# Other places for stores, modulation rows and attention parts in a transformer block on one NeuronCore

## The chip, the core and the metric

The kernel runs on one core of a Trainium2 chip. The core has five engines that run side by side: TensorE (PE, matrix products; its weight loads are listed as PEld), VectorE (DVE), ScalarE (ACT), GpSimd (POOL), and SyncE (SP), which here issues all DMAs. The metric is the device time of one execution in microseconds, less is better.

## The reference

One transformer block on 2048 tokens of 1024 channels in float32. A vector c gives six modulation rows, x is normalised and modulated, goes through a memory-augmented attention with 32 heads of 32 channels in four segments of 512 tokens, and then through a GEGLU feed-forward of 3584 channels:

```python
mod = (silu(c) @ w_mod).reshape(6, D)          # sa, ca, ga, sb, cb, gb
h = layernorm(x) * (1 + ca) + sa
q, k, v = h @ wq, h @ wk, h @ wv               # 32 heads of 32
for s in range(4):                             # segments, per head
    logits = qs @ ks.T * scale + causal_mask
    a_dot = softmax(logits) @ vs
    a_mem = (phi(qs) @ M) / (phi(qs) @ z + 1e-6)
    o = sigmoid(beta) * a_mem + (1 - sigmoid(beta)) * a_dot
    M, z = M + phi(ks).T @ vs, z + sum(phi(ks))
x = x + ga * (o @ wo)
h = layernorm(x) * (1 + cb) + sb
x = x + gb * ((gelu(h @ w_gate) * (h @ w_up)) @ w_down)
```

phi(t) is t + 1 for t > 0 and exp(t) otherwise.

## The kernel before, in words

Every large product is made of float32 numbers split into a high and a low part (`fp32r`), three matmuls for one: high by high, high by low, low by high.

**Attention** (lines 1100 to 1180) goes through 32 steps: two halves, eight groups of four heads, two segments. In step n PE works on the scores of step n, the values of step n - 1 and the projections for step n + 1 in turn. The turn is the string `ORDER` (`ORDER0` for the first): each letter lets one generator go on by one piece, V `values`, S `scores`, A `sums`, M `memory`, K `kv_part`, Q `q_part`, N the norm of the next tokens. `todo` holds work that is started at a given place of the string: loads and splits of weights, and one or two of the 32 later modulation columns a step (`mod_load`, and twelve places later `mod_col`, a multiply and sum on DVE).

Only PE's order is written out there (`manual_schedule`). For DVE, ACT, POOL and SP a planner orders the instructions by its estimates of when each is ready and by program order; each engine then runs its list in order and waits where something isn't ready. `keep_in_program_order` keeps an instruction behind everything that was traced before it on its engine.

Within a step: `q_out` (line 387) cuts q into qh on ACT and ql on DVE, `k_out` (line 367) does so for k; three DMAs each put these parts into rows 0 to 95 of `qs` and `ks`, so that one matmul makes all three products. kh, kl, qh and ql share three places of tag "sp". `scores` (line 463) makes the scores of 16 blocks, their maxima `mm` on DVE and the exponential sums `ll` on ACT; then it transposes the maxima and writes them into rows 96 to 127 of `qs` by two tensor_tensor (line 491), heads 0 and 1 on DVE, heads 2 and 3 on POOL, so that T = ks by qs in `values` (line 539) comes out with the maximum taken off. `rx`, the factor (1 - g) / sum spread over 32 channels, is a POOL tensor_tensor (line 498).

`norm_tiles` (line 238) normalises tiles of 128 tokens: statistics on DVE, the inverse root on POOL, then for name "a" (tokens 1024 to 2047, steps 1 to 10) `norm_apply` on DVE and the modulation after the transposes on DVE (line 269), for name "b" (before the feed-forward) both on ACT. Each half tile of the result is stored at once.

`row_of` (line 151) turns eight modulation columns into a row on all partitions: a diagonal on DVE, a matmul with ones, a copy on ACT, for two halves in a row. It is called for ga after step 28 and for gb after chunk 6 of pass 0.

**Feed-forward** (line 687) has three passes over tokens (768, 640, 640) with 28 chunks of 128 channels each. A chunk has seven products (a fast scheme for 2x2 blocks) of twelve matmuls; every six matmuls `step()` is called, 14 to a chunk. A step first sends what `later(n, f)` has put off by n steps and then lets each generator in `sides` go on by one piece. In pass 0, `b_part` loads the weights of the next chunk (rg, ru), makes the seven parts B and cuts each into high and low (ACT, then DVE or POOL); each B has one of eight places and is stored to HBM for the later passes with `later(6, ...)` (line 852). `wd_part` does the same for the down projection, with `later(5, ...)` (line 918). After every second chunk `down` adds the two finished chunks into `acc`. After a pass `finish` multiplies the sums by gb, adds the residual and stores, on POOL, while the next pass runs; pass 2 does this itself. From pass 0 on SP's order is also that of the program.

## Time and profile before

| | us |
|---|---|
| median of 3 runs | 3058.29 (3056.25 to 3062.48) |
| the profiled execution | 3054.25 |
| its span | 3052.5 |
| steps 1 to 19 of attention (119.0 to 712.4) | 593.4 |
| steps 20 to 27 (712.4 to 937.6) | 225.2 |
| pass 0 of the feed-forward (about 1260 to 1950) | about 690 |
| passes 1 and 2 | about 1100 |

A stage's row in the profile gives its start and end, its length, then for each engine the busy time and the number of instructions in brackets, and last the granted share of PE's clock, the busy share of the DMA engines and GB/s. A row of waits gives who waited for whom, the sum in us, the number of times and the longest. Steps are numbered from 0, and a step is counted here from its first scores to the next step's.

### The profile page before, as it was taken

The page shows a single profiled execution, that of the slowest core. Times are in us where ns is not written, and L with a number is a line of the kernel's source. Part 1 is how long each engine was busy: PE and PEld are TensorE (multiplying, and loading weights), DVE is VectorE, ACT ScalarE, POOL GpSimd, SP SyncE. Part 2 cuts the span into 40 slices and gives each one's busy share as a digit, 9 for nine tenths or more (in the row PEclk, how much of TensorE's full clock was granted, in tenths as well). Part 3 has the DMA queues.
Part 4 walks back from the last instruction along what each step waited for, and adds up shares of the span by engine and source line. Part 5 has one row for each costly group of instructions (what it writes and reads, how often), then busy time and mean ns, then how long its engine had stood idle before and what let it go on. Part 6 is the DMA issues. An engine that isn't in the chain of part 4 may idle for free.

```text
span 3052.5 us, 48071 instructions
## 1 busy us (share of the span) xinstructions
PE 2889.4 (95%) x17404; PEld 2583.4 (85%) x17404; DVE 1703.1 (56%) x3751; ACT 1136.4 (37%) x2814; POOL 919.2 (30%) x1381
## 2 busy tenths in 40 slices
PE   5999999999999997898999999999999999999998
PEld 4787778888887786788889998899999988999997
DVE  7577676766666644655656666534444353444444
ACT  5565566666666623354433333211111121111110
POOL 4444444544443513533445434411000021000000
PEclk9999999999999998999999999999999999999999
DMA  6556665564454556676878867888766668666664
GB/s 208 127 127 140 145 149 115 156 135 90 90 102 77 146 176 218 227 284 239 312 288 319 308 254 271 300 321 296 276 246 248 247 239 305 247 248 247 246 247 192
DMA packets 225852, 656.69 MB, mean 215 GB/s; under 512 B 22480, under 2 KB 59344, under 8 KB 214864
## 3 DMA queue, kind: packets, MB, share of 16 engines
q1 hardware_dynamic: 225616, 653.63, 65.4%
q8 instruction: 137, 2.24, 0.3%
q14 instruction: 99, 0.81, 0.1%
HBM read 428.10 MB, written 175.11 MB: 198 GB/s over the span
## 4 chain that ended last, share of the span: by engine, by line
PE 69%; DMA 11%; DVE 8%; POOL 3%; ACT 3%; issue 3%; SPq 1%; DVEq 0%; POOLq 0%; ACTq 0%
PE f L935 30%; PE d L970 17%; PE kv L347 8%; PE y L594 4%; PE q L353 3%; DMA qs<-qh 3%; PE S L474 2%; PE T L539 2%; PE O L548 2%; DMA ru<-wu 1%; DMA bc_d<-B 1%; POOL w L191 1%; ACT sj L478 1%; DMA ra<-h_d 1%; POOL t L726 1%
## 5 line engine op out<-in xcount | busy, mean ns | idle before, releaser
L935 PE MATMUL f<-A,B 128*128 128x320 f32 (+1 forms) x7056 | 1122.9, 319 | 31.5 <-ACT c L945 9.6
L935 PEld LDWEIGHTS f<-A,B 128*128 128x128 f32 x7056 | 1106.2, 189 | 43.0 <-DVE c L947 11.3
L970 PE MATMUL d<-wd,hc 128*128 128x512 f32 x2688 | 624.5, 392 | 6.4 <-DVE acc L1005 4.9
L970 PEld LDWEIGHTS d<-wd,hc 128*128 128x128 f32 x2688 | 505.5, 189 | 113.9 <-DVE acc L1005 6.7
L1005 DVE TENSOR_TENSOR acc<-acc,d 128x512 f32<-128x512 f32 x416 | 281.1, 685 | 184.6 <-PE d L970 181.5
L476 DVE CUSTOM_DVE_ANT_0 sj<-S,mask 128x384 f32<-128x384 f32 (+3 forms) x512 | 230.3, 488 | 207.0 <-PE S L474 198.4
L478 ACT ACTIVATE sj<-sj,mm 128x384 f32<-128x384 f32 (+3 forms) x512 | 281.5, 552 | 113.6 <-DVE mm L476 112.6
L541 ACT ACTIVATE pt<-T 128x256 f32<-128x256 f32 (+3 forms) x512 | 182.7, 446 | 93.7 <-PE T L539 88.2
L347 PE MATMUL kv<-w,hha 128*128 128x256 f32 x1024 | 211.7, 292 | 2.8 <-ACT hha L316 2.8
L347 PE MATMUL kv<-w,hhh 128*128 128x256 f32 x1024 | 203.4, 284 | 0.2 <-DVE vx L365 0.2
L542 POOL TENSOR_SCALAR_AFFINE_SELECT pt<-pt 128x128 f32<-128x128 f32 x512 | 161.7, 342 | 115.1 <-ACT pt L541 112.1
L347 PEld LDWEIGHTS kv<-w,hha 128*128 128x128 f32 x1024 | 175.0, 200 | 4.3 <-ACT hha L316 3.4
L191 POOL TENSOR_TENSOR w<-r,w 128x256 fp32r<-128x256 f32 x180 | 138.5, 801 | 104.9 <-ACT w L186 97.4
L347 PEld LDWEIGHTS kv<-w,hhh 128*128 128x128 f32 x1024 | 167.8, 192 | 2.1 <-issue 0.5
L945 ACT ACTIVATE c<-f 128x320 f32<-128x320 f32 (+1 forms) x84 | 38.2, 455 | 336.5 <-PE f L935 336.2
L956 ACT ACTIVATE c<-c 128x320 f32<-128x320 f32 (+1 forms) x84 | 41.0, 488 | 313.4 <-DVE c L955 313.4
L347 PE MATMUL kv<-w,hla 128*128 128x256 f32 x512 | 150.0, 293 | 7.4 <-POOL hla L317 6.2
L951 DVE TENSOR_TENSOR c<-f,c 128x320 f32<-128x320 f32 (+1 forms) x84 | 43.1, 513 | 200.9 <-PE f L935 200.9
L1033 POOL TENSOR_TENSOR acc<-acc,gbb 128x256 f32<-128x256 f32 x44 | 36.6, 868 | 381.0 <-DVE acc L1005 380.9
L594 PE MATMUL y<-wo,hho 128*128 128x512 f32 x384 | 130.1, 403 | 19.2 <-DVE y L599 14.4
L347 PE MATMUL kv<-w,hlh 128*128 128x256 f32 x512 | 145.1, 283 | 0.0
L474 PE MATMUL S<-ks,qs 96*128 96x256 f32 (+2 forms) x512 | 114.6, 346 | 28.6 <-DMA qs<-qh 16.7
(205 smaller groups left out, 4199.3 us busy)
## 6 DMA issues: line engine op xcount, KB each, us to landing
B<-bc_d SPq DMA_DIRECT2D x392, 512.0 KB, 6.4
bc_d<-B SPq DMA_DIRECT2D x196, 512.0 KB, 6.1
wd<-wc_d SPq DMA_DIRECT2D x56, 1024.0 KB, 6.4
wc_d<-wd SPq DMA_DIRECT2D x28, 1024.0 KB, 5.9
ks<-kh SPq DMA_DIRECT2D x64, 256.0 KB, 5.6
qs<-qh SPq DMA_DIRECT2D x64, 256.0 KB, 5.7
wm<-wmod SPq DMA_DIRECT2D x32, 512.0 KB, 4.3
r<-wkv SPq DMA_DIRECT2D x30, 512.0 KB, 5.9
```

The costliest lines, as they stand in the source:

```text
L191: eng.tensor_sub(w[:, 1, k:k + 256], r[:, k:k + 256], f32(w[:, 0, k:k + 256]))
L347: nc.tensor.matmul(ps, b[:, sl], w[:, a], start=(kt == 0 and a == 0 and b is hi), stop=(kt == KT - 1 and a == 1), **kw)
L353: nc.tensor.matmul(ps, w[:, a], b, start=(kt == 0 and a == 0 and b is hi), stop=(kt == KT - 1 and a == 1), **kw)
L474: nc.tensor.matmul(ps[:, :nk], qs[:96, j, i * P:(i + 1) * P], ks[:96, j, :nk], start=True, stop=True)
L476: nc.vector.tensor_tensor_reduce(out=sj[:, :nv], in0=ps[:, :nv], in1=mask[:, L - nv:], scale=-1.0, scalar=3.4e38, op0=ALU.add, op1=ALU.min ...
L478: nc.scalar.activation(sj[:, :nv], sj[:, :nv], AF.Exp, bias=mm[:, j, i:i + 1], scale=-1.0, accum_out=ll[:, i, j:j + 1])
L541: nc.scalar.activation(pt, ps[:, nn - n:nn], AF.Exp)
L542: nc.gpsimd.affine_select(pt[:, :P], pt[:, :P], pattern=[[1, P]], compare_op=ALU.is_ge, fill=0.0, base=0, channel_multiplier=-1)
L594: nc.tensor.matmul(ps, b[:, i * P:(i + 1) * P], w[:, a, g % 2], start=(g == 0 and a == 0 and b is hi), stop=(g == G - 1 and a == 1))
L935: nc.tensor.matmul(ps, B[m, i][:, a, kt * P:(kt + 1) * P], A[p, i, kt][b], start=(start and kt == 0 and a == 0 and b == 0), stop=(kt == 3 ...
L970: nc.tensor.matmul(ps, hid[m][:, b, tt * P:(tt + 1) * P], down_w[m][:, a, nb * L:(nb + 1) * L], start=(m == chunks[0] and a == 0 and b == ...
L1005: nc.vector.tensor_add(dst, dst, ps)
```

## The change

- In attention, line 491's two tensor_tensor become four tensor_scalar on DVE, one for each block of 128 queries, for all four heads at once. `rx` becomes an ACT copy that spreads a small product made on DVE. kh, kl, qh and ql get four places instead of three; M, mz and tt give up one each, and two constants move into temporary places.
- The norm of name "a" is normalised and modulated on ACT as "b" is; its tiles go in another rhythm (three pieces a tile, the next tile loaded one ahead, the first load before step 0). Its statistics, and the modulation columns, are pinned behind what is traced before them on DVE.
- `ORDER` is another string of 33 letters instead of 35. One column a step (two in steps 15 to 19), loaded at place 20 (and 27) and used 14 places later.
- `row_of` is split into three parts. ga's parts stand at places 4, 13 and 24 of step 29; gb's at the beginning of `finish(0)`, that is in pass 1, three steps apart.
- B and the down weights are stored 11 steps on instead of 6 and 5, and the halves of h2 that are made inside pass 0 three steps on instead of at once.

```diff
...
-    def row_of(dst, cols, tmp, name):
...
+    def row_parts(dst, cols, tmp, name):
...
+        dgs = []
         for h in range(2):
-            ps = s_ps(f"{name}{h}")
             dg = tmp(f"{name}dg{h}")
...
                                     cols[:, 4 * h:4 * h + 4].unsqueeze(2).to_broadcast([P, 4, P]), op=ALU.mult)
-            nc.tensor.matmul(ps, ones, dg, start=True, stop=True)
+            dgs.append(dg)
+        yield
+        for h in range(2):
+            ps = s_ps(f"{name}{h}")
+            nc.tensor.matmul(ps, ones, dgs[h], start=True, stop=True)
             nc.scalar.activation(dst[:, h * L:(h + 1) * L], ps, AF.Copy)
+            yield
...
+    def row_of(*a):
+        for _ in row_parts(*a):
+            pass
...
-    def mod_col(r, w):
-        nc.vector.tensor_tensor_reduce(out=w, in0=w, in1=scb, scale=1.0, scalar=0.0,
-                                       op0=ALU.mult, op1=ALU.add, accum_out=modT[:, r:r + 1])
+    def mod_col(r, w, behind=False):
+        i = nc.vector.tensor_tensor_reduce(out=w, in0=w, in1=scb, scale=1.0, scalar=0.0,
+                                           op0=ALU.mult, op1=ALU.add, accum_out=modT[:, r:r + 1])
+        if behind:
+            tc.keep_in_program_order(i)
         if r // 8 in (1, 4):
...
-    def norm_stats(halves, name):
+    def norm_stats(halves, name, behind=False):
         st = cs([P, 2, 6], "st" + name, tag="st", bufs=4)
...
         for h in range(2):
-            nc.vector.bn_stats(st[:, h], halves[h])
+            i = nc.vector.bn_stats(st[:, h], halves[h])
+            if behind:
+                tc.keep_in_program_order(i)
         nc.vector.bn_aggr(mv, st.rearrange("p a b -> p (a b)"))
...
             t = xs[q]
-            mv, rs = norm_stats([t[:, :L], t[:, L:]], f"{name}{toks[q]}")
-            if name == "b":
-                norm_scale([t], mv, rs, f"{name}{toks[q]}")
-            else:
-                norm_apply(t, mv, rs)
+            mv, rs = norm_stats([t[:, :L], t[:, L:]], f"{name}{toks[q]}", name == "a")
+            norm_scale([t], mv, rs, f"{name}{toks[q]}")
...
                 sc, sh = (modT[:, 8 * j + kt:8 * j + kt + 1] for j in (jscale, jshift))
-                if name == "b":
-                    nc.scalar.activation(hh[:, sl], ps[:, sl], AF.Identity, bias=sh, scale=sc)
-                else:
-                    nc.vector.tensor_scalar(hh[:, sl], ps[:, sl], sc, sh, op0=ALU.mult, op1=ALU.add)
-            nc.sync.dma_start(dv[:, 4 * h:4 * h + 4, tok:tok + P], hh.rearrange("p (k t) -> p k t", t=P))
+                nc.scalar.activation(hh[:, sl], ps[:, sl], AF.Identity, bias=sh, scale=sc)
+            send_h = lambda: nc.sync.dma_start(dv[:, 4 * h:4 * h + 4, tok:tok + P], hh.rearrange("p (k t) -> p k t", t=P))
+            if wait:
+                later(3, send_h)
+            else:
+                send_h()
...
                     turn(q, h)
+                    yield
+            return
+        if name == "a":
+            load(0)
+            yield
+            for q in range(len(toks) + 1):
+                if q < len(toks):
+                    stats(q)
+                yield
+                for h in range(2):
+                    if q > 0:
+                        turn(q - 1, h)
+                    if h and q + 1 < len(toks):
+                        load(q + 1)
                     yield
...
             nc.tensor.transpose(ps[:, t * P:(t + 1) * P], kn[:, t], ident)
-        kh = t2("kh" + nm, "sp", bufs=3, dt=F32R)
-        kl = t2("kl" + nm, "sp", bufs=3, dt=F32R)
+        kh = t2("kh" + nm, "sp", bufs=4, dt=F32R)
+        kl = t2("kl" + nm, "sp", bufs=4, dt=F32R)
         nc.scalar.activation(kh, ps, AF.Copy)
...
     def q_out(n, s, nm, ps):
-        qh = t2("qh" + nm, "sp", bufs=3, dt=F32R)
-        ql = t2("ql" + nm, "sp" if n else "sj", bufs=3, dt=F32R)
+        qh = t2("qh" + nm, "sp", bufs=4, dt=F32R)
+        ql = t2("ql" + nm, "sp" if n else "sj", bufs=4 if n else 3, dt=F32R)
         nc.scalar.activation(qh, ps, AF.Copy, scale=SCALE)
...
                 nc.tensor.matmul(ps[:, :P + 2], pk[:, t], vx[:, t], start=(t == 0), stop=(t == 3))
-            M = t2("Mt" + nm, "M", bufs=12, shape=(P, P + 2))
+            M = t2("Mt" + nm, "M", bufs=11, shape=(P, P + 2))
             if s == 0:
...
         nc.vector.tensor_sub(mt[:, :, :, 1], mm, f32(mt[:, :, :, 0]))
-        tt = t2("tt" + nm, "tt", bufs=2, shape=(P, P))
+        tt = t2("tt" + nm, "tt", bufs=1, shape=(P, P))
         mtf = f32(mt.rearrange("p a b c -> p (a b c)"))
...
             nc.vector.transpose(tt[96:128, 32 * a:32 * a + 32], mtf[32 * a:32 * a + 32])
-        for eng, j in ((nc.vector, 0), (nc.gpsimd, 2)):
-            eng.tensor_tensor(qs[96:128, j:j + 2].rearrange("p j (i r) -> p j i r", r=P),
-                              tt[96:128].unsqueeze(1).unsqueeze(1).to_broadcast([32, 2, 4, P]),
-                              seli[96:128].unsqueeze(1).unsqueeze(3).to_broadcast([32, 2, 4, P]), op=ALU.mult)
+        for i in range(4):
+            nc.vector.tensor_scalar(qs[96:128, :, i * P:(i + 1) * P], tt[96:128].unsqueeze(1).to_broadcast([32, 4, P]),
+                                    seli[96:128, i:i + 1], None, op0=ALU.mult)
...
         nc.vector.reciprocal(rc, ll)
+        nc.vector.tensor_mul(rc, rc, omg[:, 4 * g:4 * g + 4].unsqueeze(1).to_broadcast([P, 4, 4]))
         rx = t2("rx" + nm, "rx", shape=(P, 4, 4, DH))
-        nc.gpsimd.tensor_tensor(rx, rc.unsqueeze(3).to_broadcast([P, 4, 4, DH]),
-                                omg[:, 4 * g:4 * g + 4].unsqueeze(1).unsqueeze(3).to_broadcast([P, 4, 4, DH]), op=ALU.mult)
+        nc.scalar.activation(rx, rc.unsqueeze(3).to_broadcast([P, 4, 4, DH]), AF.Copy)
         SC[n] = [rx, None]
...
             M = Mst[g, s - 1]
-            mz = t2("mz" + nm, "mz", bufs=2, shape=(P, P + 4))
+            mz = t2("mz" + nm, "mz", bufs=1, shape=(P, P + 4))
             nc.vector.tensor_mul(mz[:, :P], M[:, :P], blk)
...
                 k = (fc * 7 + i - 1) * P
-                later(6, lambda: nc.sync.dma_start(bc_d[k:k + P], f32(t.rearrange("p a b -> p (a b)"))))
+                later(11, lambda: nc.sync.dma_start(bc_d[k:k + P], f32(t.rearrange("p a b -> p (a b)"))))
                 B[m, i] = t
...
                     yield
-            later(5, lambda: nc.sync.dma_start(wc_d[m * P:(m + 1) * P], f32(w.rearrange("p a b -> p (a b)"))))
+            later(11, lambda: nc.sync.dma_start(wc_d[m * P:(m + 1) * P], f32(w.rearrange("p a b -> p (a b)"))))
             down_w[m] = w
...
+            if p == 0:
+                row = row_parts(gbb, modT[:, 40:48], tmp_tile, "gb")
+                for _ in range(3):
+                    next(row)
+                    for _ in range(3):
+                        yield
             residual(0)
...
                     sides.append([a_mix(2), 1, "m"])
-                if m == 6:
-                    row_of(gbb, modT[:, 40:48], tmp_tile, "gb")
                 pend.append(m)
...
     steps = [(hf, g, s) for hf in range(2) for g in range(G) for s in (2 * hf, 2 * hf + 1)]
-    ORDER = "K V K V N K K V N V V V K S K N S K V V V S K A S N Q M K Q V V Q K Q"
+    ORDER = "K N V K V K N K V N V V V K K S K S Q V V V S K A S Q M K Q Q V V"
     ORDER0 = "N N N N N N N N K S K K S S K A S K K K K Q Q M K Q Q"
...
         norm_a = norm_tiles(x, hT_d, (2, 3), 1, 0, "a")
+        next(norm_a)
         for n in range(len(steps) + 1):
...
             if rest and n > 0:
-                for pos in (5, 21)[:1 + n % 2]:
+                for pos in (20, 27)[:1 + (15 <= n < 20)]:
                     got = []
                     todo.append((pos, lambda r=rest.pop(0), got=got: got.append(mod_load(r))))
-                    todo.append((pos + 12, lambda got=got: mod_col(*got[0])))
+                    todo.append((pos + 14, lambda got=got: mod_col(*got[0], behind=True)))
             for pos, q in enumerate((ORDER if n else ORDER0).split()):
...
                 gab = t2("gab", "row", shape=(P, D))
-                row_of(gab, modT[:, 16:24], tmp_tile, "ga")
+                ga_row = row_parts(gab, modT[:, 16:24], tmp_tile, "ga")
+                todo += [(at, lambda: next(ga_row)) for at in (4, 13, 24)]
         pa_close()
...
```

4 lines of the change are left out of this document (2 added, 2 removed).

## The prediction

> **What bounds the kernel now.** I read the page first, then the busy times by stage, then TensorE's waits inside each stage, and last the chain of waits and the queue of SyncE at single stalls.
>
> ```profile
> span 3052.5 us, 48071 instructions
> ...
> PE 2889.4 (95%) x17404; PEld 2583.4 (85%) x17404; DVE 1703.1 (56%) x3751; ACT 1136.4 (37%) x2814; POOL 919.2 (30%) x1381
> ...
> PEclk9999999999999998999999999999999999999999
> ```
>
> PE is the bound, busy in 95% of the span, so the change can only win time in which PE stands still, runs spread out, or runs at a lower granted clock. Where that is, the busy times by stage tell. The first two rows count all instructions, the next two only the score matmuls (line 474, 16 to an attention step).
>
> ```profile
> 119.00:712.40 593.40, 560.15 (x3988) 476.36 (x3988) 416.76 (x1221) 366.25 (x1064) 271.62 (x487) 0.98 0.59 133
> 712.40:937.60 225.20, 224.31 (x1665) 194.44 (x1665) 146.04 (x460) 154.15 (x448) 98.33 (x200) 1.00 0.49 95
> ```
>
> ```profile
> 119.00:712.40 593.40, 68.98 (x304) 47.95 (x304) 0.98 0.59 133
> 712.40:937.60 225.20, 27.16 (x129) 19.46 (x129) 1.00 0.49 95
> ```
>
> 304 scores are 19 steps, 128 are 8 (one more reaches over the edge). A step takes 593.40/19 = 31.23 us in the earlier stage and 225.20/8 = 28.15 us in the later one, where the norm of tokens 1024 to 2047 and most modulation columns are done. The surplus is 3.08 x 19 = 58.5 us, the largest sum that this change can reach. PE's waits in the earlier stage:
>
> ```profile
> PE S L474 <- issue: 9.4, 6, 2.7
> PE S L474 <- DMA qs<-qh: 9.1, 8, 2.4
> PE T L539 <- DVE ry L521: 6.6, 5, 1.8
> PE T L539 <- DVE qs L491: 3.5, 5, 1.5
> ```
>
> Scores wait 18.5 us for q and k parts, T waits 10.1 us for VectorE. The granted clock of 0.98 costs another 0.02 x 593.4 = 11.9 us. One score wait, from the chain of waits (start, duration, what):
>
> ```profile
> 226.34 2.79 DVE qs L491
> ...
> 231.51 1.23 DVE wm L179
> ...
> 233.21 1.20 DVE sta L222 x2
> ...
> 236.23 0.69 DVE ql L391
> ...
> 236.94 4.37 DMA qs<-ql
> ...
> 243.10 0.71 PE S L474 x4
> ```
>
> The low part of q, ql, is made at 236.23, behind 9.9 us of other DVE work: the maxima rows, a modulation column, the statistics and the normalisation of a tile. Its DMA then lands just before the scores start.
>
> **Attention, the norm and the columns: -28 us.** Durations of what is removed, added and moved (minimum/median/maximum ns; the first is the tensor_tensor that goes, the second the tensor_scalar nearest to the four that come):
>
> ```profile
> L491 DVE TENSOR_TENSOR qs<-tt,seli x32: 1467/2793/2828, 93.3 to 1049.6; 32x1024 fp32r<-32x1024 f32 x32
> L382 DVE TENSOR_SCALAR ek<-ek x24: 363/420/1296, 63.8 to 991.1; 128x512 f32<-128x512 f32 x24
> L236 DVE TENSOR_SCALAR na<-na,mva,rsa x8: 811/814/815, 103.8 to 334.6; 128x1024 f32<-128x1024 f32 x8
> L269 DVE TENSOR_SCALAR hta<-tpa,modT x64: 396/405/412, 181.4 to 421.1; 128x128 f32<-128x128 f32 x64
> L233 ACT ACTIVATE nb<-nb,mrb,rsb x16: 1236/1243/1246, 1106.9 to 1538.9; 128x1024 f32<-128x1024 f32 x16
> L267 ACT ACTIVATE htb<-tpb,modT x128: 438/457/492, 1129.3 to 1551.4; 128x128 f32<-128x128 f32 x128
> L568 ACT ACTIVATE R<-R x32: 569/577/599, 124.5 to 1071.2; 128x512 f32<-128x512 f32 x32
> ```
>
> Maxima rows: DVE now takes 2.79 us in the median for half of the heads. Afterwards it does all heads with four tensor_scalar of 512 elements each, which no row shows with this broadcast; the bounds are 4 x 0.363 = 1.5 and 4 x 1.296 = 5.2 us, and I take the median of the nearest row, 4 x 0.42 = 1.7. POOL loses its half and rx; rx becomes an ACT copy of 0.58 us (bounds 0.57 and 0.60, same shape). The small product of rc and omg has 16 columns and is lost in DVE's idle time.
>
> On the path of the quoted stall: maxima rows -1.1 us; the column (1.23 us) is pinned behind what is traced before it, and at place 20 + 14 of a step of 33 places it comes behind ql; so do the statistics, which with the wait for POOL fill 233.21 to 236.23 (3.0 us). ql comes 1.1 + 1.2 + 3.0 = 5.3 us earlier, against waits of 2.7 us at most. Besides, the last q product moves from the last of 35 places to place 30 of 33 and the first scores from place 13 to 15, with one more piece of k and v between them. So I count all 18.5 us of the score waits as gone. The fourth place for q and k parts works in the same direction and gets no gain of its own. Of the T waits I take half, 5 us, since ry stays on DVE while qs gets shorter. Of the clock's 11.9 us I take 8, as low clock follows stalls (shown below). Together 31.5 us.
>
> What comes back: 64 modulations and 8 normalisations go to ACT, 64 x 0.457 + 8 x 1.243 = 39.2 us over nine steps; with rx that is 4.9 us a step more, on 366.25/19 = 19.3 us. ACT is then busy for 24.2 of some 29.6 us, while DVE, at 416.76/19 = 21.9, is relieved of 64 x 0.405 + 8 x 0.814 = 32.4 us. An exponential behind a normalisation waits 1.2 us; I charge 0.4 us in each of nine steps, 3.5 us. Net -28 us, bounds -58.5 (all surplus) and +25 (no wait goes, half of ACT's 50 us of added work, 39.2 + 19 x 0.58, lands on PE). The columns that move into the later steps cost
>
> ```profile
> L179 DVE CUSTOM_DVE_ANT_0 wm<-wm,scb x32: 1209/1222/1753, 90.4 to 675.7; 128x1024 f32<-128x1024 f32 x32
> ```
>
> 1.2 us of DVE each, one a step for eight steps, where DVE is idle for 35%: zero, at most 8 x 1.3 = 10 us if the cover is gone.
>
> [...] The rows of L491 (1467 to 2828 ns) and L382 agree that something doubles or triples an instruction. [...]
>
> **The two modulation rows: -6 and -10 us.** PE's waits around step 28 and in pass 0 of the feed-forward, and the stages of halved clock that follow (the last three numbers are granted clock, DMA share, GB/s):
>
> ```profile
> PE ga L158 <- DVE gadg L156: 4.5, 1, 4.5
> ...
> 959.00:962.40 3.40, 3.40 (x5) 1.18 (x5) 1.82 (x3) 0.60 (x1) 0.34 (x1) 0.50 1.04 137
> ```
>
> ```profile
> PE gb L158 <- DVE gbdg L156: 7.6, 2, 6.9
> PE f L935 <- DVE c L947: 7.2, 6, 1.6
> PE d L970 <- DVE acc L1005: 4.9, 1, 4.9
> ```
>
> ```profile
> 1409.60:1419.80 10.20, 6.72 (x11) 3.54 (x12) 4.07 (x7) 4.84 (x11) 4.82 (x7) 0.50 0.91 313
> ...
> 1573.40:1580.20 6.80, 5.24 (x12) 4.13 (x13) 5.29 (x8) 2.25 (x4) 5.95 (x8) 0.50 0.72 225
> ```
>
> Both rows keep their DVE products, matmuls and copies; what goes is PE's wait, because the diagonals are made places ahead of the matmuls. ga: 4.5 us and half of 3.4 us at halved clock, 6 us. gb: 7.6 and half of 10.2, 12.7 us; but DVE itself is held up there, and the down projection behind it needs DVE after four PSUM places, so I take 10 (bounds 7.6 and 12.7). In pass 1 the row delays the last residual work by nine steps, hidden by the 42 steps (three chunks) before the first accumulators are wanted again; I allow 3 us, three steps, if it isn't.
>
> [...]
>
> **Stores later: -6 us.** The queue of SyncE in pass 0, its waits and one stretch:
>
> ```profile
> SPq L852 <- DVE B L722: 161.6, 65, 7.6
> SPq L270 <- ACT htb L267: 72.7, 20, 11.2
> ```
>
> ```profile
> 1539.47 0.32 SPq L852 DMA_DIRECT2D bc_d<-B  x1
> 1550.14 0.37 SPq L270 DMA_DIRECT2D h_d<-htb  x1
> ```
>
> SP waits in order. From 1539.8 to 1550.1 it stood at a store of h2, with the loads of the next weights behind it; these came late, DVE with them, and PE then waited 4.9 us at the accumulator and ran 6.8 us at halved clock: 8.3 us. With h2's stores three steps and B's eleven steps on, a chunk's loads pass two of its seven B stores and such h2 stores. I take 6 of 8.3 us (bounds 0 and 8.3).
>
> But a store also frees one of eight places for B. A step is half a product; landing takes 6.1 us:
>
> ```profile
> 1588.62 29.14 PE f L935 x168
> ...
> bc_d<-B SPq DMA_DIRECT2D x196, 512.0 KB, 6.1
> ```
>
> 168 matmuls are 28 steps, so a step is 1.04 us. In program order the place was wanted 9 to 11 steps after the store was sent; now it is 4 to 6, or 5.2 us, a little less than the landing. The parts are cut about eleven steps before use, which covers that: nothing gained, nothing lost on the 7.2 us of c (bounds -7, and +25 for 0.9 us in each of 28 chunks).
>
> **The sum:** -28 - 6 - 10 - 6 = -50 us from the profiled execution's 3054.25 us, 3004 us. That execution lies 4 us under the median of the runs shown, so on their scale 3008 us.
>
> **The rivals.**
>
> Everything fits: every step falls to 28.15 us and all stalls go, 58.5 + 6.2 + 12.7 + 8.3 = 86 us, 2973 us. For it speaks that the later steps reach this with the same engines; against it, ACT's 24 us.
>
> ACT takes DVE's place in the norm's steps, the exponentials come late and the score waits turn into T and O waits. Attention then gives nothing, 22 us stay: 3036 us. For it: 39.2 us on ACT in nine steps; against it, DVE was loaded as highly on average and lost only through the order of its work.
>
> Slower: places for B run out. ACT's cut waits for a store's landing, and the copies of PSUM behind it on ACT and DVE wait too, then PE. The six waits at c L947 show that there is little slack. If half of the 5.2 us reaches PE in each of 28 chunks, 73 us come on top, the 6 us of the stores don't come: 3058 - 44 + 73 = 3087 us. It decides from 44/28 = 1.6 us a chunk.
>
> The change doesn't do what it says: only PE's order is written out in attention, and the planner may put the norm or the stores back on the path of ql. Then attention loses about what ga and gb win, 3058 us.
>
> **How the numbers follow.** Chances: the forecast 0.45, everything fits 0.15, ACT 0.20, B places 0.12, no effect 0.08. The predicted time is the forecast's, 3008 us. The range 2982 to 3054 us holds the forecast with its bounds and ACT, and leaves out the slower rival and half of the fastest. What this kernel's measurement can tell from no change is about 0.2%, 6 us; faster 0.82 (the first three and a little of the last), within it 0.05, slower 0.13.
>
> **What would show it.** Right: earlier attention steps of 29.5 to 30 us, score waits under 4 us there, ql right behind the maxima rows, no halved clock near the two rows, no SP wait of 10 us at h2's stores. Wrong: ACT above 85% busy in the first nine steps with T or O waiting for it; waits of PE for c that grow with the chunks of pass 0; DVE waiting for columns' DMAs; steps 20 to 27 longer than 28.5 us.

## The result, and the profile after

The changed kernel takes 2981.32 us (median, 2979.85 to 2985.15), the kernel before beside it 3057.27 us: a ratio of 0.975, 95% interval 0.9733 to 0.9767, or 76 us less. The forecast was 50 us less, 3008 us; the result lies 0.7 us under the lower end of the range. Its page, and its busy times by stage for steps 1 to 19, 20 to 27 and 28 to 30 of the attention:

```profile
span 2978.9 us, 47962 instructions
...
PE 2872.2 (96%) x17404; PEld 2566.1 (86%) x17404; DVE 1633.7 (55%) x3815; ACT 1181.3 (40%) x2918; POOL 804.9 (27%) x1317
```

```profile
113.92:674.64 560.72, 548.64 (x3991) 463.12 (x3989) 364.29 (x1228) 403.86 (x1154) 199.49 (x450) 1.00 0.64 134
674.64:911.58 236.94, 232.04 (x1666) 196.19 (x1665) 149.79 (x508) 158.54 (x456) 81.19 (x184) 0.99 0.53 110
911.58:1001.30 89.72, 87.92 (x598) 71.65 (x597) 63.23 (x201) 62.30 (x176) 38.27 (x76) 1.00 0.59 116
```

Steps 1 to 19 are 32.7 us shorter than before (593.40), but steps 20 to 27, which stood at 225.20, are 11.7 us longer. PE's waits in the two stages:

```profile
PE T L563 <- DVE qs L516: 3.5, 4, 1.2
PE T L563 <- ACT hta L276: 3.4, 8, 0.5
PE T L563 <- DVE kl L400: 2.2, 5, 0.6
PE T L563 <- DVE ry L545: 2.0, 5, 0.5
```

```profile
PE T L563 <- DVE qs L516: 2.3, 4, 0.6
PE T L563 <- DVE kl L400: 1.3, 4, 0.3
PE T L563 <- DVE ry L545: 1.3, 4, 0.3
```

The score waits of 18.5 us are gone; those of T are not, and they are now in the later stage too. In pass 0 the win lies in two stretches, chunks 4 to 6 and chunks 10 to 13, before and after:

```profile
1340.63:1434.66 94.03, 85.59 (x428) 75.31 (x426) 56.26 (x96) 38.88 (x79) 38.19 (x46) 0.95 0.82 296
...
1499.71:1603.04 103.33, 96.46 (x499) 88.58 (x498) 62.45 (x98) 39.76 (x79) 48.20 (x57) 0.97 0.84 303
```

```profile
1297.12:1377.05 79.93, 79.48 (x424) 73.29 (x423) 52.34 (x89) 36.69 (x76) 36.76 (x45) 1.00 0.87 319
...
1440.46:1534.07 93.61, 93.15 (x499) 87.02 (x498) 59.26 (x94) 39.39 (x81) 47.03 (x56) 1.00 0.78 288
```

14.1 and 9.7 us, the first with the gb row in it, and PE's granted clock is 1.00 in both, after 0.95 and 0.97.

### The profile page after: what moved, and what is told of

The parts are those of the page before. It is cut to its first block, busy times and chain, and to the rows that moved or that the text cites. A ratio compares the mean times of both kernels' runs of the same rounds, so it can differ in the third digit from the quotient of the medians.

```text
span 2978.9 us, 47962 instructions
## 1 busy us (share of the span) xinstructions
PE 2872.2 (96%) x17404; PEld 2566.1 (86%) x17404; DVE 1633.7 (55%) x3815; ACT 1181.3 (40%) x2918; POOL 804.9 (27%) x1317
## 4 chain that ended last, share of the span: by engine, by line
PE 76%; DVE 8%; DMA 7%; issue 3%; POOL 3%; ACT 3%; SPq 0%; DVEq 0%; POOLq 0%; ACTq 0%
PE f L959 32%; PE d L994 18%; PE kv L372 9%; PE q L378 3%; PE y L618 3%; PE T L563 3%; PE S L499 2%; PE O L572 2%; DMA ra<-h_d 1%; DVE qs L516 1%; POOL t L750 1%; POOL w L202 1%; DMA B<-bc_d 1%; DMA ru<-wu 1%; DVE A L746 1%
## 5 line engine op out<-in xcount | busy, mean ns | idle before, releaser
L566 POOL TENSOR_SCALAR_AFFINE_SELECT pt<-pt 128x128 f32<-128x128 f32 x512 | 169.9, 354 | 324.0 <-ACT pt L565 318.8
L202 POOL TENSOR_TENSOR w<-r,w 128x256 fp32r<-128x256 f32 x180 | 133.0, 772 | 171.2 <-ACT w L197 152.6
L563 PEld LDWEIGHTS T<-qs,ks 128*128 128x128 f32 x512 | 81.5, 190 | 86.9 <-issue 35.1
L563 PE MATMUL T<-qs,ks 128*128 128x256 f32 (+2 forms) x512 | 131.1, 362 | 20.3 <-DVE qs L516 6.4
```

Of the source, the lines that this page charges most:

```text
L202: eng.tensor_sub(w[:, 1, k:k + 256], r[:, k:k + 256], f32(w[:, 0, k:k + 256]))
L563: nc.tensor.matmul(ps[:, :nn], ks[:, j, kc * P:(kc + 1) * P], qs[:, j, L - nn:], start=True, stop=True)
L566: nc.gpsimd.affine_select(pt[:, :P], pt[:, :P], pattern=[[1, P]], compare_op=ALU.is_ge, fill=0.0, base=0, channel_multiplier=-1)
```

## The experiments

All times below are in us: the median, the 95% interval of the ratio to the kernel before, and from the profiled execution the length of stages, each from its first matmul (of the scores, or of the first gate and up product of a chunk) to the next one's. So chunks 4-6 end where chunk 7 begins, and the expectations call this stretch chunks 4 to 7, likewise 10 to 14. "Old order" is the changed kernel with the string `ORDER` of before.

| kernel | median | ratio | steps 1-19 | 20-27 | 28-30 | chunks 4-6 | 7-9 | 10-13 |
|---|---|---|---|---|---|---|---|---|
| before | 3057.3 | 1 | 593.4 | 225.2 | 97.1 | 94.0 | 65.0 | 103.3 |
| changed | 2981.3 | 0.9733-0.9767 | 560.7 | 236.9 | 89.7 | 79.9 | 63.4 | 93.6 |
| old order | 2963.3 | 0.9681-0.9707 | 557.0 | 224.3 | 86.4 | 79.9 | 63.4 | 93.7 |
| columns early | 2988.5 | 0.9761-0.9787 | 563.1 | 235.8 | 89.7 | 79.9 | 63.4 | 93.7 |
| q split late | 2984.6 | 0.9744-0.9782 | 560.9 | 235.7 | 91.0 | 79.9 | 63.4 | 93.6 |
| q piece last | 2990.1 | 0.9767-0.9794 | 575.7 | 226.6 | 88.7 | 79.9 | 63.4 | 93.6 |
| old order, maxima rows and rx back | 3002.1 | 0.9801-0.9838 | 576.9 | 230.4 | 93.3 | 79.9 | 63.4 | 93.8 |
| old order, maxima rows back | 2999.2 | 0.9795-0.9826 | 574.9 | 231.1 | 91.8 | 79.9 | 63.4 | 93.7 |
| before with new maxima rows and rx | 3032.9 | 0.9910-0.9935 | 579.7 | 223.8 | 96.5 | 94.5 | 63.7 | 103.0 |
| old order, norm on DVE | 2958.8 | 0.9659-0.9697 | 548.4 | 224.1 | 86.4 | 79.9 | 63.4 | 94.1 |
| the same, statistics not pinned | 2966.5 | 0.9685-0.9721 | 549.1 | 224.1 | 86.4 | 79.9 | 63.4 | 93.6 |
| old order, norm wholly as before | 2984.5 | 0.9749-0.9776 | 571.5 | 224.2 | 86.4 | 79.9 | 63.4 | 93.6 |
| old order, norm on DVE, columns from step 7 | 2967.3 | 0.9691-0.9728 | 556.5 | 224.0 | 86.4 | 79.9 | 63.4 | 93.6 |
| old order, columns back | 2978.7 | 0.9718-0.9760 | 563.5 | 223.6 | 86.4 | 79.9 | 63.4 | 93.7 |
| old order, three places | 2971.3 | 0.9704-0.9731 | 564.0 | 224.0 | 88.6 | 79.9 | 63.4 | 94.0 |
| all stores back | 2998.1 | 0.9795-0.9822 | 560.9 | 237.0 | 89.7 | 80.2 | 64.0 | 99.9 |
| B's stores back | 3003.6 | 0.9802-0.9830 | 560.4 | 235.8 | 89.7 | 82.8 | 66.5 | 99.6 |
| h2's stores back | 3003.1 | 0.9807-0.9834 | 560.4 | 235.8 | 89.8 | 85.4 | 70.0 | 98.7 |
| gb row back | 2990.3 | 0.9767-0.9794 | 560.6 | 237.1 | 89.7 | 83.4 | 62.7 | 93.6 |
| gb row and stores back | 3018.7 | 0.9860-0.9887 | 560.9 | 234.6 | 91.0 | 92.5 | 64.9 | 102.1 |

The table also tells how finely stages can be read: with the same attention, steps 1 to 19 repeat within 0.5 us (560.4 to 560.9) and with the same pass 0, chunks 4 to 6 within 0.1. Other stretches do not: from the scores of step 31 to the first chunk the changed kernel takes 208.1 us and the one that differs only in the gb row, much later, 212.9 us; and chunks 0 to 2 of pass 1 take 53.8 to 63.5 us in kernels that differ in the attention alone. So a difference of totals under some 10 us is read from the stages.

### The longer steps 20 to 27: columns or order

The columns that now stand there:

```diff
-for pos in (20, 27)[:1 + (15 <= n < 20)]:
+for pos in (20, 27)[:1 + (7 <= n < 20)]:
```

> The changed kernel with two modulation columns a step from attention step 7 on instead of step 15, so that all 32 are done by step 19 and none is left for steps 20 to 27. Changed kernel: steps 20 to 27 take 236.9 us (225.2 before), and the even ones, which carry a single column and the cut of new weights for k and v, 30.8 to 32.0. Theory (the column's load takes a raw place that the weights of k and v need, these come late, and their cut falls beside the maxima rows and ahead of the copy of rx on ACT): steps 20 to 27 go back to 225 to 229 us, steps 7 to 14 grow by 2 us at most in all, total 2969 to 2975 us. Rival (the order of the pieces and rx on ACT make the even steps long, columns or not): steps 20 to 27 stay above 234 us, total 2978 to 2984 us. Second rival (columns cost PE wherever they are): steps 7 to 19 grow by what steps 20 to 27 lose, total 2978 to 2984 us too, told apart by the stages.

The eight columns have left (DVE 16 instructions and 9.7 us less, two instructions to a column), and the stage falls by 1.1 us, no more than it differs between kernels with the same attention (234.6 to 237.1). The theory falls: the columns cost nothing there, and the rival of the order is left. (The total rises by 7.2 us to 2988.5, above every range given; 2.4 us of the rise lie in steps 1 to 19, the rest outside the stages that the edit touches.)

```diff
-ORDER = "K N V K V K N K V N V V V K K S K S Q V V V S K A S Q M K Q Q V V"
+ORDER = "K V K V N K K V N V V V K S K N S K V V V S K A S N Q M K Q V V Q K Q"
```

> The changed kernel with the order of the pieces of an attention step as it was before (35 places instead of 33, four pieces of the norm a step instead of three, scores from place 13, the last q product at place 35); normalisation on ACT, maxima rows, rx, four places, columns and rows as in the changed kernel. Theory (the score waits went because q's low part comes earlier and the scores come later; the order does about half of that): score waits of 8 us or more come back in steps 1 to 19, which grow from 560.7 us by 10 to 20 us; total 2990 to 3003 us. Rival (the maxima rows without POOL and the fourth place did it, the order is worth nothing): steps 1 to 19 within 4 us of 560.7, total 2978 to 2986 us. Second rival (the new order causes the longer steps 20 to 27): these fall below 230 us.

The theory falls and the second rival holds: the new order costs 18 us (2963.3 against 2981.3), 12.6 of them in steps 20 to 27 and 3.3 in steps 28 to 30, and wins nothing in steps 1 to 19, which fall by another 3.7 with the old one. The same place of step 22 in the timelines (start, duration, engine, line), first with the new order, then with the old:

```profile
745.11 2.96 POOL L202 TENSOR_TENSOR w<-r,w 128x256 fp32r<-128x256 f32 x4 [4.39 <-ACT w L197]
...
746.50 0.77 DVE L509 CAST mt<-mm 128x16 fp32r<-128x16 f32 x1
...
747.38 0.71 DVE L510 TENSOR_TENSOR mt<-mm,mt 128x16 fp32r<-128x16 f32 x1
...
749.31 1.06 ACT L197 ACTIVATE w<-r 128x1024 fp32r<-128x1024 f32 x1 [0.98 <-PE q L378]
749.51 2.17 DVE L516 TENSOR_SCALAR qs<-tt,seli 32x512 fp32r<-32x512 f32 x4
750.45 3.19 POOL L202 TENSOR_TENSOR w<-r,w 128x256 fp32r<-128x256 f32 x4 [2.38 <-ACT w L197]
...
752.42 0.56 DVE L521 TENSOR_TENSOR rc<-rc,omg 128x16 f32<-128x16 f32 x1
...
753.02 0.63 ACT L523 ACTIVATE rx<-rc 128x512 f32<-128x512 f32 x1 [2.65 <-DVE rc L521]
```

```profile
741.48 1.70 DVE L516 TENSOR_SCALAR qs<-tt,seli 32x512 fp32r<-32x512 f32 x4
...
744.00 0.17 DVE L521 TENSOR_TENSOR rc<-rc,omg 128x16 f32<-128x16 f32 x1
...
744.20 0.63 ACT L523 ACTIVATE rx<-rc 128x512 f32<-128x512 f32 x1 [2.76 <-DVE rc L521]
...
745.22 1.05 ACT L197 ACTIVATE w<-r 128x1024 fp32r<-128x1024 f32 x1
...
746.35 2.22 POOL L202 TENSOR_TENSOR w<-r,w 128x256 fp32r<-128x256 f32 x3 [6.50 <-PE T L563]
```

The split of the next q weights (L197 on ACT, L202 on POOL) overwrites the weights of the running q product, so the end of that product (`<-PE q`) lets it go. In the new order that is four places earlier, and the split runs beside the maxima rows and what follows them on DVE; from the rows to rx it takes 3.5 us instead of 2.7, and q's high part and T's exponentials stand behind rx on ACT. Two more things differ. The rows start later, 15.0 us after the step's first scores instead of 13.5: the two small instructions on the maxima ahead of them (`mt`), beside POOL's split of weights for k and v, take 0.77 and 0.71 us instead of 0.26 and 0.18. And PE comes to T earlier, 16.5 us after the first scores instead of 18.0, because one piece of k and v that lay between now comes ahead of the scores. So it waits there for the rows, kl and ry; the waits of 4.9 us listed above for steps 20 to 27 are those of the four even steps, which hold these splits. Two edits try what the split does. The first asks for the split later:

```diff
-(26, 0, 0), (37, 1, 0)])
+(26, 0, 0), (42, 1, 0)])
```

> The changed kernel, its own order of pieces kept, with the split of the next q weights asked for at place 42 instead of 37, five places later in the step after. Changed kernel 2981 us, steps 20 to 27 236.9 us, with the old order of pieces 224.3 us and 2963 us in all. Theory (the new order ends the q product four places earlier and is two places shorter, so the split of the next q weights on ACT and POOL comes beside the maxima rows instead of behind them; the fourth of these then takes 0.95 us instead of 0.48, the small product for rx 0.57 instead of 0.17, and ACT holds q's high part and the T exponentials behind rx): steps 20 to 27 fall to 224 to 229 us, total 2966 to 2973 us. Rival (the new order itself, scores spread out and the last q product nearer to the scores, makes the even steps long): steps 20 to 27 stay above 234 us, total 2977 to 2984 us. Second rival (the late split makes the next q product wait): the odd steps get longer and the total is above 2984 us.

Nothing moves (235.7), but the trace shows the split still right behind the end of the q product, so the edit did not make the case it was meant for and tells nothing. The second moves what releases the split, the end of the q product:

```diff
-"... V V V K K S K S Q V V V S K A S Q M K Q Q V V"
+"... V V V K K S K S V V V S K A S Q M K Q Q V V Q"
```

> The changed kernel with one piece moved: the first of the four q pieces of an attention step goes from place 18 to the last place, so that the q product ends behind everything else, as in the old order; the other 32 pieces stay. Changed kernel 2981 us, steps 20 to 27 236.9 us; asking for the split of the next q weights five places later left both unchanged, and the split still ran right behind the end of the q product. Theory (the end of the q product releases the split, which then falls beside the maxima rows): the split comes behind the maxima rows, the fourth of them takes 0.48 us again, steps 20 to 27 fall to 224 to 229 us, steps 1 to 19 stay within 5 us, total 2966 to 2974 us. Rival (the rest of the new order, scores from place 15 and spread wider, makes the even steps long): steps 20 to 27 stay above 234 us, total 2977 to 2985 us. Second rival (a q product that ends late makes scores wait again): score waits of more than 5 us in steps 1 to 19 and a total above 2985 us.

```profile
689.58:916.14 226.56, 226.07 (x1666) 193.97 (x1665) 148.32 (x508) 155.52 (x456) 78.05 (x184) 1.00 0.54 113
```

```profile
PE T L563 <- ACT pt L565: 8.0, 10, 1.7
PE T L563 <- ACT hta L276: 6.6, 14, 0.7
```

Steps 20 to 27 are back at 226.6 us by moving one piece of 33: its early place made them long. That the split beside the rows does it, as the theory has it, is not shown. In step 22 the split of weights for k and v now lies beside the rows, which take 2.64 us, longer than in the changed kernel; from the rows to rx it takes 3.7 us, and still PE does not wait. The move did two things at once. The q split comes 1 us behind the start of rx. And the scores lie closer together without the q piece between them, and `mt` is ready before the other split begins, so the rows start at 12.1 us of the step instead of 15.0, while PE comes to T at 16.5 us in both. The odd steps of the changed kernel have the early q piece but no such splits, and take 27.8 us, against 27.5 with the old order. So the loss needs the early piece and the splits together, and how it divides between the late rows and the slowed instructions stays open. Steps 1 to 19 grow by 15 us, with T waiting for ACT where the normalisation is; scores wait for 3.9 us, less than the 5 of the second rival, so it is right that a late q piece costs, and wrong on the place.

### The maxima rows

```diff
-for i in range(4):
-    nc.vector.tensor_scalar(qs[96:128, :, i * P:(i + 1) * P], ...)
+for eng, j in ((nc.vector, 0), (nc.gpsimd, 2)):
+    eng.tensor_tensor(qs[96:128, j:j + 2]..., ...)
```

In the first kernel rx goes back to POOL with them, in the second it stays on ACT; the third adds both new edits alone to the kernel before.

> The changed kernel with the old order of pieces (2963 us, steps 1 to 19 557.0 us, 20 to 27 224.3 us), and besides with the maxima rows as two tensor_tensors on DVE and POOL and rx on POOL, as before. What remains of the change in the attention: normalisation on ACT, four places, the columns' places. Theory (the maxima rows at 1.7 instead of 2.8 us bring ql forward and end most score waits): steps 1 to 19 grow by 8 to 20 us, score waits come back, total 2971 to 2985 us. Rival (the gain of the earlier steps is DVE's relief from the normalisation, or the columns' places): steps 1 to 19 grow by less than 5 us, total 2960 to 2969 us.

> The changed kernel with the old order of pieces (2963 us), and the maxima rows alone again as two tensor_tensors on DVE and POOL; rx stays on ACT. With both back it took 3002 us. Theory (the maxima rows carry it: beside POOL they take 2.8 us, and POOL's half stands behind its splits of weights): total 2988 to 3004 us. Rival (rx on POOL, behind the maxima rows' half there, was the cause): total 2963 to 2975 us.

> The kernel before, with the four tensor_scalars for the maxima rows and with rx on ACT, and nothing else of the change. Kernel before 3056 us; steps 1 to 19 593.4 us, 20 to 27 225.2 us. Taking these two edits out of the changed kernel with the old order cost 39 us (2963 to 3002 us), 19.9 of them in steps 1 to 19 and 6.1 in steps 20 to 27. Theory (these two carry most of what the attention won, whatever stands around them): steps 0 to 30 fall by 20 to 40 us, total 3016 to 3036 us. Rival (they only help where the normalisation has left DVE, or with the fourth place): steps 0 to 30 fall by less than 10 us, total 3046 to 3058 us.

By the medians 36 of the 39 us are the maxima rows'. About 7 of these 36 lie in chunks 0 to 2 of pass 1 (61.6 us after 54.3), which the edit does not touch; the stages give the rows 30 us (17.9, 6.8 and 5.4) and both edits 33. The row of the line, below it the time for which ACT stood idle in front of rx until rc was there, and PE's largest wait in steps 1 to 19, with the rows taken back:

```profile
L516 DVE TENSOR_TENSOR qs<-tt,seli x32: 1220/2794/2805, 91.2 to 1025.3; 32x1024 fp32r<-32x1024 f32 x32
```

```profile
  DVE rc L522: 103.2, 31
```

```profile
PE T L564 <- ACT pt L566: 8.8, 9, 1.7
```

and with the four tensor_scalars:

```profile
L516 DVE TENSOR_SCALAR qs<-tt,seli x128: 478/480/489, 92.6 to 998.4; 32x512 fp32r<-32x512 f32 x128
```

```profile
  DVE rc L521: 69.7, 31
```

The rows are 1.1 us longer, and what is behind them is late in each step: rc, rx, the exponentials of T. ACT's idle time before rx alone is 33.5 us longer, and T's wait for ACT's exponentials was 1.1 us with the four tensor_scalars. In the old form the two halves run side by side, and the one that starts second is the long one. In the kernel before, POOL's half starts 0.15 to 0.4 us ahead in 30 of the 32 steps and takes 1.89 us, DVE's 2.6 to 2.8; in the other two DVE's starts 0.5 us ahead and takes 1.47 to 1.48 us, POOL's 2.76 to 2.77. Either way 3.0 to 3.2 us pass from the first start to the last end. With the rows taken back here the medians are the same, 2.79 us on DVE and 1.89 on POOL. No run has a half alone. In the kernel before, the two edits win 24.6 us, 13.7 in steps 1 to 19, but its score waits stay:

```profile
PE S L474 <- DMA qs<-qh: 14.1, 10, 2.5
PE S L474 <- issue: 7.4, 4, 3.0
```

21.5 us against 18.5 before. So the rows are the largest part of the gain over all attention steps, and not by ending the score waits.

### What ended the score waits: norm, columns, fourth place

All on the old order. First the norm's two computations back on DVE, then its rhythm and loads as before too, and then only the pinning of its statistics taken out:

```diff
-norm_scale([t], mv, rs, ...)                      # and the modulation on ACT
+norm_apply(t, mv, rs)                             # and the modulation on DVE
```

> The changed kernel with the old order of pieces (2963 us), and besides with the normalisation and the modulation of tokens 1024 to 2047 on DVE again; the rhythm of its pieces stays new. Theory (39.2 us moved from DVE to ACT take what stood ahead of ql out of its way): steps 1 to 8 grow by 6 to 16 us, total 2968 to 2980 us. Rival (ACT pays as much as DVE gains, as the forecast charged it in part): steps 1 to 8 stay within 4 us, total 2960 to 2967 us. Second rival (ACT is what keeps steps 1 to 6 at 30 us instead of 28): they fall by 5 us or more, total below 2959 us.

> The changed kernel with the old order of pieces (2963 us), and the norm of tokens 1024 to 2047 wholly as before: normalisation and modulation on DVE, loads and turns in the old rhythm of four pieces a tile, statistics not held in program order. With only the two computations back on DVE it takes 2959 us, steps 1 to 19 548.4 us. Theory (the statistics in front of ql were what made the scores wait, the new rhythm puts them behind it): score waits of 6 us or more come back, steps 1 to 19 take 560 to 580 us, total 2970 to 2990 us. Rival (the norm's rhythm is worth nothing): steps 1 to 19 548 to 556 us, total 2957 to 2967 us.

> The changed kernel with the old order of pieces and the norm's computation on DVE (2959 us, steps 1 to 19 548.4 us), its statistics no longer held in program order; its rhythm of three pieces a tile stays. With the old rhythm and no such order it took 2984 us, steps 1 to 19 571.5 us. Theory (the order keeps the statistics behind ql; without it DVE takes them as soon as their tile has landed): total 2973 to 2988 us. Rival (the rhythm carries it, the order changes nothing): total 2956 to 2963 us.

The row of steps 1 to 19, first with the computations on DVE in the new rhythm, then with all as before, and PE's waits of the scores in the latter:

```profile
116.21:664.56 548.35, 541.48 (x3990) 464.87 (x3989) 386.26 (x1292) 374.92 (x1083) 197.76 (x450) 1.00 0.64 137
```

```profile
118.34:689.88 571.54, 550.11 (x3990) 471.06 (x3989) 390.05 (x1287) 374.17 (x1082) 196.06 (x445) 0.99 0.61 130
```

```profile
PE S L491 <- issue: 4.9, 5, 3.3
PE S L491 <- DMA qs<-qh: 4.4, 2, 2.2
...
PE S L491 <- DMA na<-x: 2.6, 1, 2.6
```

With the old order, having this work on ACT loses 8.6 us in steps 1 to 19 (557.0 against 548.4), as the second rival had it. But 5.4 of them lie in step 6 alone (36.1 against 30.7 us), where ACT stands 3.0 us for the load of the next q weights, because their split is next in its list, and the exponential sums, the maxima and PE's scores wait behind it. Step 6 of the changed kernel has no such stall (29.7 us), so what the move costs there is not shown. The rhythm of three pieces a tile with its earlier loads, with about the same work on each engine, wins 22.4 us (571.5 against 549.1 without pins), and with the old one 11.9 us of score waits are back. The pinning wins 0.7 us there, so the theory that it carries the gain falls; the total without it lies between the two expectations, with step 0 3.5 us longer and the first chunks of pass 1, which it does not touch, 9.4. The fastest kernel of all comes out of this, 2958.8 us, though its interval overlaps that of the old order alone. Holding the columns back from the norm's steps was meant to add to it:

```diff
-for pos in (20, 27)[:1 + (15 <= n < 20)]:
+for pos in (20, 27)[:2 * (7 <= n < 20) + (n >= 20)]:
```

> The changed kernel with the old order of pieces and the normalisation and modulation on DVE (2959 us; DVE busy 24 of 30 us in steps 2 to 6, 17 of 28 from step 7), and the modulation columns held back until step 7, two a step up to step 19 and one in each of six steps more. Theory (a column of 1.2 us beside the norm on DVE costs PE part of it): steps 1 to 6 fall by 3 to 7 us, the later ones stay, total 2951 to 2957 us. Rival (columns are behind ql and cost nothing in steps 1 to 6): total 2957 to 2963 us.

It loses 8.1 us in steps 1 to 19 instead, outside both expectations. 7.7 of these lie in step 14, where T waits 3.0 us for the rows and the next scores 1.4 us for a load of normalised tokens; why both are late there stays open. The columns at their places of before, and three places instead of four:

```diff
-for pos in (20, 27)[:1 + (15 <= n < 20)]:     # product 14 places on, pinned
+for pos in (5, 21)[:1 + n % 2]:               # product 12 places on
```

> The changed kernel with the old order of pieces (2963 us), and besides with the modulation columns at places 5 and 21 (product 12 places on, not held in program order, two in the odd steps from step 1) as before. Theory (the column's product of 1.2 us stood ahead of ql and is now behind it): steps 1 to 19 grow by 6 to 15 us, total 2968 to 2979 us. Rival (columns are hidden wherever they are): within 4 us, total 2959 to 2967 us.

```diff
-kh = t2("kh" + nm, "sp", bufs=4, dt=F32R)     # and kl, qh, ql
+kh = t2("kh" + nm, "sp", bufs=3, dt=F32R)
```

> The changed kernel with the old order of pieces (2963 us, steps 1 to 19 557.0 us, no score waits for q's parts), and three places for q and k parts instead of four. Theory (the fourth place ended the score waits: with three, the new k's and q's parts wait for the DMAs out of the old ones): score waits of 8 us or more come back, steps 1 to 19 grow by 8 to 25 us, total 2972 to 2990 us. Rival of the forecast (the fourth place gains nothing of its own): within 4 us, total 2959 to 2967 us.

These cost 6.5 and 7.0 us in steps 1 to 19, at and just under the lower ends that the theories gave. The scores wait for q's parts by 2.0 us again with the columns and, issue included, by 4.2 us with three places, half of what the theory asked for; the rest of the loss is spread out. The parts do not add up: taken back one by one, the maxima rows, the rhythm, the columns and the fourth place lose more in steps 1 to 19 (17.9, 22.4, 6.5, 7.0) than the 36.4 us that the old order wins over the kernel before with all of them.

### Stores and the gb row

```diff
-later(11, lambda: nc.sync.dma_start(bc_d...   # B; wd alike
+later(6, lambda: nc.sync.dma_start(bc_d...    # wd: 5
-later(3, send_h)                              # h2
+send_h()
```

All three stores back, B's alone, h2's alone, the gb row alone (`row_of` after chunk 6 again), and the row with all stores:

> The changed kernel with its three stores back where they were before: B's stores 6 steps behind the cut, the down weights' 5, and h2's halves sent at once. Changed kernel: 2981 us. Theory (the stores hold SyncE up, and the next weights' loads queue behind them): the stall of pass 0 around its chunks 10 to 14 comes back, where the changed kernel is 9.7 us shorter than the one before; up to 3 us more in the last chunks of the attention's projections and at the start of pass 1. Total 2989 to 2995 us, and SyncE stands again for some 10 us at a store of h2. Rival (the shorter pass 0 is gb's row and the rhythm that follows from it, the stores are hidden anyway): chunks 10 to 14 stay as in the changed kernel and the total is 2979 to 2984 us. Second rival (the later stores cost places for B): the total falls below 2979 us.

> The changed kernel with B's stores alone 6 steps behind the cut again; h2's halves and the down weights' stores stay late. Changed kernel 2981 us, with all three stores back 2998 us. Theory of the forecast (the stall came from h2's store, which held SyncE for 10 us; B's stores matter little): total 2979 to 2986 us. Rival (B's stores, on which SyncE stands for some 177 us in 73 waits when they come early, hold up the loads): total 2990 to 3000 us. Second rival (late B stores cost places for B): total below 2977 us.

> The changed kernel with h2's halves sent at once again, B's and the down weights' stores late. Changed kernel 2981 us; with B's stores alone early 3004 us, with all three early 2998 us. Forecast's theory (the store of h2 that held SyncE for 10 us cost 8.3 us in chunks 10 to 14): that part of pass 0 grows by 4 to 9 us, total 2985 to 2990 us. Rival (with B's stores late the queue has slack and h2's stores are hidden): total 2979 to 2984 us.

> The changed kernel with gb's row made in one go after chunk 6 of pass 0 again. Theory (the row itself holds PE up, 7.6 us of wait and half of 10.2 us at halved clock): chunks 4 to 7 are 12 to 15 us longer than in the changed kernel, nothing is won in pass 1, total 2992 to 2996 us. Rival (most of the 14.1 us by which chunks 4 to 7 became shorter are the stores', which no longer hold up the loads beside the row): chunks 4 to 7 are less than 7 us longer, total below 2988 us.

> The changed kernel with both gb's row in one go after chunk 6 of pass 0 and the three stores at their old places. Chunks 4 to 7 take 94.0 us before, 79.9 in the changed kernel, 83.4 with the row alone put back and 80.2 with the stores alone put back. Theory (the row's wait needs the queue held up by the stores to become long, the two edits overlap): chunks 4 to 7 take 90 to 95 us, total 3005 to 3015 us. Rival (the two add up and the rest of the 14.1 us is due to the start of pass 0 being another): chunks 4 to 7 take 83 to 86 us, total 2999 to 3007 us.

SyncE's waits in pass 0, in the changed kernel, with all stores back, with B's and with h2's:

```profile
SPq L876 <- DVE B L746: 31.3, 24, 3.7
SPq L277 <- ACT hc L744: 31.1, 5, 9.9
```

```profile
SPq L873 <- DVE B L743: 175.8, 71, 6.4
SPq L277 <- ACT htb L276: 71.3, 20, 11.3
```

```profile
SPq L876 <- DVE B L746: 210.4, 66, 14.2
```

```profile
SPq L277 <- ACT htb L276: 138.2, 20, 21.3
```

Either kind of store, sent early, holds the queue up by itself: B's for 210 us, h2's for 138. In chunks 4 to 13 one kind alone back costs more than all of them (12.0 and 17.2 against 7.2 us). Over the whole of pass 0 B's cost 9.9 us, h2's 14.0 and all three 14.2 (677.9, 682.0 and 682.2 after 668.1), so the costs of the two kinds do not add up. The medians differ by 22 us for either kind and by 17 for all, but chunks 0 to 2 of pass 1 are part of that: 61 us with either kind back, 54.5 in the changed kernel and 52.3 with all. All three totals lie above what any theory gave. The gain needs all of them late: h2's are not the sole cause, as the forecast had it, and not hidden, as the rival had it.

With the row alone back, chunks 4 to 6 are 3.5 us longer, as the rival of the row's own price had it (the total of 2990.3 us is 2 us above its range), with the stores alone 0.3, with both 12.6: the theory of an overlap holds, though the total is 4 us above its range. The row's wait in the two kernels, first with late stores, then with early ones:

```profile
PE gb L162 <- DVE gbdg L156: 1.5, 1, 1.5
```

```profile
PE gb L162 <- DVE gbdg L156: 7.6, 2, 6.9
```

How the one makes the other, from SyncE's waits between 1375 and 1393 us of the kernel before and from its chain of waits:

```profile
SPq L270 <- ACT htb L267: 11.1, 2, 10.3
```

```profile
1389.87 1.41 ACT htb L267 x4
...
1391.29 0.37 SPq L270
...
1393.02 1.22 SPq L844
...
1394.30 7.61 DMA ru<-wu
...
1409.73 1.79 POOL B L722 x2
...
1411.55 0.70 DVE gbdg L156
...
1412.30 2.09 PE gb L158 x2
```

The stores of two halves of h2 (L270) wait for ACT, the first for 10.3 us; the loads of the next gate and up weights (L844) queue behind it on SyncE, ru lands late, the B part made of it on POOL is late, DVE's diagonal for gb waits for that, and PE stands. The row was the place where the stores' delay became visible.

## Why the prediction was right in direction and too small

**Pass 0 is the step that failed.** The forecast priced the gb row and the stores as two separate terms, 10 and 6 us. Its stores step, 6 of 8.3 us, was bounded by one stall at the accumulator in chunks 10 to 13. In chunks 4 to 13 (the last three columns) the stores are worth 7.2 us with the gb row late (244.1 less 236.9) and 19.8 with the row where it was (259.5 less 239.7). Its gb step, 10 us with 7.6 to 12.7 for bounds, credits the row with what was in part the same thing: with late stores the row is worth 2.8 us (239.7 less 236.9), with early ones 15.4. Together they are 22.6 us there, against the 16 of the forecast. Over the whole of pass 0 both taken back cost 24.9 us (692.9 after 668.1) of the 28.1 by which the changed kernel shortened it (696.2 to 668.1), and the stores alone 14.2. The missing step was to follow back the wait for gb's diagonal, whose chain led to the very store queue that the stores step priced elsewhere.

**Places for B** were costed at nothing with 25 us at stake; that was right. Chunks 14 to 27 take 343.4 us after 342.1, and the late stores lose nothing.

**Attention: the sum fits, its terms do not.** Steps 1 to 19 win 32.7 us where 28 were forecast, at 29.5 us a step, with no score wait, ACT at 72% and PE's clock at 1.00. But:

- The maxima rows are sized right, four in 1.70 us where POOL is quiet (forecast 1.7), and their place is not: the 1.1 us were put on ql alone, as one of three helps against 18.5 us of score waits. They stand ahead of T in each step, and are worth 30 us in the attention's stages when taken out with the old order.
- The forecast's upper bound for the four, all at 1.296 us, did not come: the median of 128 is 0.48. But in 12 of the 32 steps of the changed kernel they take 2.2 to 3.1 us together, with POOL's splits beside them (line 202 in ten, line 225 in two), and 1.7 us in the other 20, where POOL works beside them for 0.2 us in one step and not at all in the rest. The product of 16 columns takes 0.56 to 0.59 us in the 11 steps with a split of line 202 beside it and 0.16 to 0.18 in the others. Why these instructions are longer there is not shown.
- The norm on ACT was counted as relief for DVE and charged 3.5 us; with the old order it loses 8.6 us net, most of it in one stall. What wins is the rhythm of its pieces, 22.4 us, which the forecast had only as statistics that come behind ql.
- The fourth place was given nothing and is worth 7 us. The new order was counted as a help and costs 18.
- T's waits, of which half were to go, remain: 7.7 us for DVE and 3.4 for the modulation on ACT, after 10.1.

**Steps 20 to 27** were costed at zero, at most 10 us, for the columns. They cost 11.7 us, the sign that the forecast named (29.6 us a step, over 28.5), but the cause is the order: a piece of q placed early makes the rows late, lets the split of the next q weights run beside them and leaves PE at T before they are done. The prediction looked at what the order does to the scores, and not at what it does to T, nor at what the end of a product releases. This loss hid part of the gain; otherwise the miss would have been larger.

**The ga row** fits: steps 28 to 30 fall by 7.4 us (forecast 6), without the wait for its diagonal (4.5 us before) and without a halved clock (1.00 in the stage's row, after 0.50 for 3.4 us). No run takes this row back alone, and the order and the maxima rows act there too.

**Where nothing was counted** lie another 17.3 of the 73.6 us by which the profiled spans differ, more than the 12.1 by which pass 0 exceeds its 16: 5.1 before step 1, 6.2 between the scores of step 31 and the first chunk, 6.0 in passes 1 and 2. Step 0 alone takes 35.6 to 42.0 us in the kernels of the table, and the last two are no more than such stretches differ between kernels without an edit there. So no cause is claimed for these 17.3 us. They and the 11.7 us lost in steps 20 to 27 were both unforeseen and partly cancel; that the total came so near the range is luck to that extent.

## What to carry to other kernels

Before a wait is priced, follow its chain back to the first thing that stood still: two waits with different names can be one held-up queue, and then the parts do not add up. In an order written out by hand, look at what each product's end releases on the other engines as well as at what its start needs; and judge an instruction on DVE by everything that is queued behind it in each step, not by the one wait that first showed it.

## What the runs showed beyond the expected

Beside POOL's split, in step 22, some of DVE's smallest instructions grow most in proportion, against the same step with the old order: a product of 16 columns takes 0.56 instead of 0.17 us and a cast of 16 columns 0.77 instead of 0.26, while four tensor_scalars of 512 together go from 1.70 to 2.17 us and a reciprocal of 16 columns stays at 0.25. And the same code does not take the same time in another kernel: chunks 0 to 2 of pass 1 took 53.8 to 63.5 us in kernels that differ in attention only, a spread of 9.7 us where the runs of the changed kernel spread over 5.3; what sets it stayed open.
